# Sliding-window attention with a highway layer behind it: V's odd tiles copied to the other row half, PV in one phase, a narrower last stage, more biases by ScalarE, and a new order of steps

## The chip, the cores and the metric

The kernel runs on one core of a Trainium2 chip. The metric is device time in microseconds, from launch to end, of one execution. The engines are named as in the profile: PE (TensorE, matmuls), PEld (its weight loads), DVE (VectorE), ACT (ScalarE), POOL (GpSimd), SP (SyncE, which here only issues DMAs).

## The reference

Eight batches, eight heads, 576 positions, head width 64. Each query sees itself and the 127 keys before it, with a linear bias by distance that differs by head. The result of all heads, 4608 rows of 512, goes through a highway layer.

```
scores = (q @ k.T) / sqrt(64) - slope[h] * (i - j)       # where 0 <= i - j < 128
attn   = softmax(scores)                                  # else masked out
x      = (attn @ v), heads side by side                   # 4608 x 512
H      = relu(x @ w_h)
T      = sigmoid(x @ w_t + b_t)
out    = T * H + (1 - T) * x
```

## The kernel before, in words

**Steps and order.** The whole program is a string, `ORDER`, of three-character steps: a letter for the kind of step and a number for the item. A loop at the end reads it and emits the instructions of each step, under a manual schedule, so every engine gets its own instructions in the order in which the string names them. A second string, `BANKS`, gives the PSUM bank of each new accumulator (eight banks of 512 floats; `take`).

**Loading.** `L` steps load q and k of four heads of one batch (`ld..`), as bfloat16, from POOL's queue: four loads a batch (two groups of heads, k and q), 288 KB each. `V` loads V of a batch in 64-wide rows with a column of ones beside them (`va`, 576 KB), `W` the weights and the bias row, `B` the bias on all 128 rows (`bA`). A `T` step is one VectorE transpose of a load into `tr..`, so that the head width lies on 32 rows, two elements deep.

**Attention.** A batch has four stages; stage s holds the key tiles 2s and 2s+1 of 64 keys each, for all eight heads, and the fourth also tile 8. `s` computes the scores: 32 matmuls of 32 rows by 64 columns with 192 queries moving, and in the fourth stage 16 more of 32 by 128 with 64 queries. `e` is the exponential on ACT, from PSUM to bfloat16; `m` multiplies it on DVE by a table that holds both the distance bias and the mask (`mk`). In the probabilities the two tiles of a stage lie in different row halves, and which one is where alternates with the head, as V's rows do in memory (nine tiles a head). PV therefore runs in two phases: `p` for the even tiles, `y` (or `Y`, with a drain of PE ahead of it) for the odd ones, where the row halves change places. An output block is 128 queries; blocks of index NS hold the last 64 queries of two batches. `n` divides by the sum that the column of ones gave (a reciprocal and a multiply, on DVE).

**Highway layer.** For each of 36 blocks: `x` transposes the block on PE, `c` copies it to SBUF on ACT, `h` and `z` are four matmuls each with the two weights. The bias of the gate comes either by one more matmul at the end of `z` (L393), or by a copy of `bA` into the bank ahead of it on ACT (step `b`, 12 of the 36 blocks). `u` computes relu(h) - x on DVE; `U` is the relu on ACT and then needs `v`, the subtraction on DVE. `a` is a tanh on ACT; `t` (ACT) or `D` (DVE) turns it into the gate; `g` (DVE) or `G` (POOL) multiplies; `o` (POOL) or `O` (DVE) adds x; `d` stores from SP's queue. A POOL step of that kind waits for the DVE operation that the string names last before it.

Of the kernel before, what the change touches and what calls it, by code (L numbers as in the profile page):

```python
# [14 lines left out]
ADD = ()  # L15
# [3 lines left out]
    "Q00L00B00R00S00L01r00L02L03J00k00P00K00L04L05L06L07T00V00T01W00L08T02I00W01T03s00W02T04s"  # L19
    "01e00L09T05e01s02V01T06e02s03T07e03L10m00s04m01s05e04m02L11m03p00e05p01Y00Y01n00p02L12n0"  # L20
    "1x00Y02c00p03n02x01V02h00c01m04x02y03c02h01n03U00s06m05L13x03L14e06z00T08h02c03T09a00s07"
    "t00v00z01u01e07g00m06h03U02p04m07a01p05Y04t01Y05n04z02U03G01b03n05z03L15a02T10V03x04p06a"
    "03T11p07c04Y06t02Y07n06z04o01n07s08a04D03x05v02e08x06D04x07T12h04c05s09v03c06m08h05c07T1"
    "3G03e09z05u04G02h06U05T14a05s10o00b06p08T15e10Y08o03d00z06d01n08U06L16s11m09a06x08e11m10"
    "h07v05z07u07o02c08s12a07m11L17d02p09d03e12p10Y09Y10G04n09t05s13n10L18p11e13o04T16Y11x09x"
    "10L19c09n11d04s14c10V04h08m12e14h09m13U08s15m14b08h10e15g05T17o05z08u10z09a08d05v06t06m1"
    "5p12a09p13Y12t07x11n12U09z10G07c11T18t09x12y13o07a10p14p15n13Y14b11Y15L20c12v08p16n14t10"
    "G06z11n15h11a11o06T19x13x14c13y16L21d06p17c14n16d07L22x15h12L23c15D11g10U11s16D08U12g08y"
    "17v09z12e16n17G09T20x16h13a12o08c16s17b14u13z13L24d08e17v11L25m16z14t12T21o10p18a13s18a1"
    "4m17L26Y18t13h14n18e18G13z15T22o09U14p19a15s19b16v12V05d09Y19m18e19d10z16n19h15o13T23a16"  # L30
    "x17x18c17p20L27g12U15T24Y20G11c18s20z17n20e20o11T25h16o12t15d11s21a17u16x19e21d12h17D14v"
    "14d13m19h18U17z18c19T26G14U18x20m20L28h19a18c20D16s22T27b19G16p21e22Y21u19o14z19n21s23L2"
    "9v15d14a19m21L30p22e23h20g15D17z20m22U20v17x21m23p23c21p24y22a20Y23n22o15z21n23o16d15p25"
    "a21y24Y25t18n24G17p26d16t19x22n25h21c22L31v18x23x24U21v20y26g19x25b22D20h22g18c23g20n26o"
    "17z22t21c24u22h23V06a22d17v21c25s24T28U23z23e24O19h24D22O18a23m24s25d18b24d19h25e25v23D2"
    "3z24G23u25U24T29x26z25G22c26a24T30s26o20a25z26e26T31d20h26m25a26s27U26g21m26p27e27p28Y27"
    "Y28v24n27o21t24n28s28V07d21x27e28v26p29g24x28m27Y29c27s29c28n29o22h27e29h28m28d22U27p30o"
    "23u28s30b27Y30e30o24d23x29n30z27c29v27d24s31m29a27z28e31m30h29D26D25g26a28g25p31m31p32t2"
    "8x30z29c30D27U29g28g27p33a29o25y31y32n31h30b30n32d25x31z30c31O28p34O26a30y33Y34U30D29d26"
    "n33p35t30h31v29g29x32z31v30c32n34o29b32x33u31y35c33x34o27n35z32a31g30h32d27a32D31d28g31c"  # L40
    "34d29z33O30t32O31d30U32x35h33a33d31v32c35g32z34D33U33O32v33h34d32a34g33h35t34u34z35O33U3"
    "5g34d33v35O34a35D35d34g35O35d35"
)
BANKS = (
    "1404040642740106057405613572357067450674075047506406540540567507256320742534074507640674"
    "0671450740574357045064520326105307546054067150750640754076407605730625723310567540271570"
    "1"
# [3 lines left out]
def lists():  # L51
# [16 lines left out]
    by.update({k: blocks for k in "pynxchuvbzatgod"})  # L68
# [4 lines left out]
def kernel(  # L73
# [38 lines left out]
    TR = {(i, g, w): cp.tile([P, SQ, 2], BF16, name=f"tr{i}{g}{w}")  # L112
          for i in range(2) for g in range(NG) for w in "qk"}
    va = cp.tile([P, NB, NV, D + 1], BF16, name="va")
    VA = [va[:, i] for i in range(NB)]
    PB = [cp.tile([P, NH, 576], BF16, name=f"p{i}") for i in range(NP)]
    PE3 = [cp.tile([P, NH, 576], BF16, name=f"r{i}") for i in range(NP3)]
# [5 lines left out]
    MK = cp.tile([P, NH, 2, 192], BF16, name="mk")  # L123
    MA = cp.tile([P, NH, 2, 192], BF16, name="ma") if ADD else None
    MK3 = cp.tile([P, NH, 2, 256], BF16, name="mk3")
# [6 lines left out]
    scaled = [None]  # L132
# [4 lines left out]
    def between(ins, last=None):  # L137
        last = last or paired[0]
        if last is not None:
            tc.add_manual_dep(  # L140
                ins.ins, last.name,
                mybir.DependencyInfo(mybir.DependencyClass.Sync, mybir.DependencyReason.DATA),
                reason="starts behind VectorE's last operation on the shared port")
# [22 lines left out]

    def zero(ap):
        nc.vector.memset(ap.bitcast(U32), 0)  # L168

    def pads(i):  # L170
        for g in range(NG):
            for w in "qk":
                zero(TR[i, g, w][:, S:SQ, :])

    def clear(step):
        if step == "J":
            zero(spin[:])
        elif step == "R":
# [3 lines left out]
            pads(0)  # L182
        elif step == "P":
            for p in PB:
                for c in (0, 256, 512):
                    zero(p[:, :, c : c + 64])
        else:
            zero(ones0[:])
            nc.vector.memset(ones0[0:1, :], 1.0)
            for p in PE3:  # L190
                zero(p[:, :, 0:64])
            zero(MK3[:, :, :, 192:256])
            pads(1)
# [5 lines left out]
    def setup(step):  # L199
# [14 lines left out]
        elif step == "k":  # L214
            for tab in (MK, MK3):
                for h in range(NH):
                    for g in range(NG):
                        nc.scalar.activation(out=tab[:, h, g, 0:192], in_=rel[:], func=ACTF.Exp,
                                             scale=-slopes[4 * g + h])
            for half in range(2):  # L220
                rows = slice(half * D, (half + 1) * D)
                nc.scalar.copy(out=MK3[rows, half::2, :, 192:256], in_=MK[rows, half::2, :, 0:D])
        else:
            nc.sync.dma_start(
                out=bA[:], in_=moe_b_t.rearrange("(o n) -> o n", o=1).broadcast_to([P, DM]))

    def additive():
        for h in range(NH):
            for g in range(NG):
                nc.scalar.activation(out=MA[:, h, g, :], in_=rel[:], func=ACTF.Copy,  # L230
                                     scale=-slopes[4 * g + h] / scale)

    def tr(w, b, g):
        nc.vector.transpose(
            out=TR[b % 2, g, w][:, 0:S].rearrange("p s e -> p (s e)").bitcast(U32).rearrange(
                "p (s t) -> p t s", t=NT),
            in_=LD[b % 2, g, w][:].bitcast(U32).rearrange("p (t i) -> p t i", i=32))

# [15 lines left out]
    def scores(b, s):  # L254
# [3 lines left out]
        pitch = 192 if s < 3 else 256  # L258
        add = (b, s) in ADD
        for h in range(NH if add else 0):  # L260
            nc.tensor.matmul(
                out=sc[:, h, 0:384], lhsT=ident[:],
                rhs=MA[:, h].rearrange("p g n -> p (g n)"), start=True, stop=False)
        for g in range(NG):
            for e in range(2):
                for i in range(2):
# [35 lines left out]
    def terms(b, s, i):  # L302
        if s == NS:
            return [(3, 6, 128), (3, 8, 192)] if i == 0 else [(3, 7, 64)]
# [173 lines left out]
```

## Time and profile before

| | |
|---|---|
| median of 3 runs | 156.6 us (156.53 to 159.39) |
| the profiled execution | 156.13 us, of which the span is 154.2 |
| mean granted clock of PE | 0.976 |
| busy in the span: PE, DVE, ACT, POOL | 130.4, 136.0, 121.3, 80.8 us |
| DMA packets | 48106, 25.30 MB, 38224 of them under 512 B |
| last DVE operation ends / span ends | 149.9 / 154.2 us |

The profile counts an engine as busy while an instruction of it is under way; neighbours may overlap at their ends, so the distance from one start to the next is often shorter than an instruction. An idle time is named after what ended it. "Landing" is the time from the issue of a DMA to its completion.

### The profile page before, as it was taken

The numbers are of one execution on the slowest core, as the hardware profiler recorded it, in microseconds if no ns is written. First come the engines' busy times: TensorE is split into PE (matmuls) and PEld (weight loads), VectorE is DVE, ScalarE is ACT, GpSimd is POOL, SyncE is SP. The second block draws the span as 40 slices with busy tenths as digits, with TensorE's granted clock in tenths as the row PEclk, the third lists the DMA queues.
The fourth block names the chain that finished last, engine by engine and source line by source line (L and its number), as shares of the span: only waits on it lengthen the run. The fifth ranks groups of instructions, "written<-read, shape, count | busy, mean of one in ns | idle before, by whom it ended". The sixth has DMA issues, their size and how long they took to land.

```text
span 154.2 us, 6207 instructions
## 1 busy us (share of the span) xinstructions
PE 130.4 (85%) x2694; PEld 71.8 (47%) x2728; DVE 136.0 (88%) x257; ACT 121.3 (79%) x178; POOL 80.8 (52%) x90
## 2 busy tenths in 40 slices
PE   0598658698998999998999999989999799999930
PEld 0233326344554555465545545466445554555410
DVE  4999948398999899997999999989999979999880
ACT  3655972299579999994999999868999999868830
POOL 6984414402909479279488957554753771204000
PEclk9999995999999999999999999999999999999995
DMA  4999999999999759997999998786599199042732
GB/s 70 197 206 207 161 198 210 160 196 167 189 175 65 197 107 204 189 185 142 127 223 231 221 183 232 137 161 168 101 129 229 68 133 233 6 138 108 302 136 68
DMA packets 48106, 25.30 MB, mean 164 GB/s; under 512 B 38224, under 2 KB 39248, under 8 KB 48080
## 3 DMA queue, kind: packets, MB, share of 16 engines
q0 software_dynamic: 42688, 15.21, 91.6%
q1 hardware_dynamic: 5392, 9.70, 18.5%
q8 instruction: 21, 0.34, 0.9%
q14 instruction: 5, 0.04, 0.1%
HBM read 30.67 MB, written 9.44 MB: 260 GB/s over the span
## 4 chain that ended last, share of the span: by engine, by line
PE 70%; DMA 10%; issue 6%; DVE 6%; ACT 5%; DVEq 0%
PE ps L389 19%; PE ps L362 19%; PE ps L333 14%; DMA va<-in_v_dram 10%; PE ps L269 8%; PE ps L352 6%; PE ps L393 3%; ACT r L293 2%; ACT p L293 1%; DVE ot L417 1%; PE ps L279 1%; DVE p L168 1%; DVE uu L412 0%; DVE x L343 0%; ACT tt L402 0%
## 5 line engine op out<-in xcount | busy, mean ns | idle before, releaser
L417 POOL TENSOR_TENSOR ot<-uu,x 128x512 f32<-128x512 bf16 x26 | 29.8, 1155 | 23.8 <-DVE uu L376 9.6
L293 ACT ACTIVATE p<-ps 128x1536 bf16<-128x1536 f32 x24 | 34.7, 1457 | 4.6 <-PE ps L269 4.3
L362 PE MATMUL ps<-wH,xt 128*128 128x512 bf16 x130 | 35.3, 382 | 1.6 <-issue 1.0
L389 PE MATMUL ps<-wT,xt 128*128 128x512 bf16 x127 | 35.4, 380 | 1.1 <-issue 0.3
L412 POOL TENSOR_TENSOR uu<-uu,tt 128x512 bf16<-128x512 bf16 x14 | 16.1, 1153 | 23.8 <-ACT tt L402 10.6
L357 ACT COPY xt<-ps 128x512 bf16<-128x512 bf16 x36 | 20.6, 587 | 9.9 <-PE ps L352 9.7
L397 ACT ACTIVATE tt<-ps 128x512 f16<-128x512 f32 x36 | 21.6, 602 | 7.0 <-PE ps L393 4.7
L343 DVE TENSOR_TENSOR x<-ps,rd 128x512 bf16<-128x512 f32 x36 | 24.9, 691 | 2.1
L333 PE MATMUL ps<-va,p 64*128 64x65 bf16 x768 | 22.2, 193 | 3.9 <-DMA va<-in_v_dram 1.3
L300 DVE TENSOR_TENSOR p<-p,mk 128x1536 bf16<-128x1536 bf16 x24 | 22.8, 970 | 0.0
L333 PEld LDWEIGHTS <-p 64*128 64x128 bf16 x768 | 16.6, 95 | 12.6 <-issue 10.2
L362 PEld LDWEIGHTS <-xt 128*128 128x128 bf16 x144 | 13.0, 99 | 14.2 <-issue 1.8
L389 PEld LDWEIGHTS <-xt 128*128 128x128 bf16 x144 | 12.6, 98 | 12.9 <-issue 0.6
L154 POOL DMA_DIRECT2D va<-in_v_dram x8 | 14.8, 1851 | 1.9 <-DMA ld00k<-in_k_dram 1.0
L293 ACT ACTIVATE r<-ps 128x2048 bf16<-128x2048 f32 x8 | 15.0, 1874 | 0.5
L372 ACT ACTIVATE uu<-ps 128x512 bf16<-128x512 f32 x24 | 14.4, 604 | 1.0 <-PE ps L362 0.9
L352 PE MATMUL ps<-ident,x 128*128 128x128 bf16 x144 | 13.7, 225 | 1.5 <-issue 1.2
L342 DVE RECIPROCAL rd<-ps 128x8 f32<-128x8 f32 x36 | 7.1, 198 | 7.6 <-PE ps L333 7.1
L352 PEld LDWEIGHTS <-x 128*128 128x128 bf16 x144 | 9.5, 99 | 6.3 <-issue 1.9
L402 ACT ACTIVATE tt<-tt 128x512 f16<-128x512 f16 x19 | 11.9, 632 | 0.1
L242 PE MATMUL ps<-spin 128*128 128x512 bf16 x22 | 7.2, 503 | 5.4 <-DVE spin L168 5.4
L300 DVE TENSOR_TENSOR r<-r,mk 128x2048 bf16<-128x2048 bf16 x8 | 10.3, 1294 | 0.3 <-ACT r L293 0.3
(77 smaller groups left out, 195.2 us busy)
## 6 DMA issues: line engine op xcount, KB each, us to landing
out_dram<-ot SPq DMA_DIRECT2D x32, 256.0 KB, 4.0
va<-in_v_dram POOLq DMA_DIRECT2D x8, 576.0 KB, 10.9
ld00k<-in_k_dram POOLq DMA_DIRECT2D x4, 288.0 KB, 5.7
ld00q<-in_q_dram POOLq DMA_DIRECT2D x4, 288.0 KB, 6.0
ld01k<-in_k_dram POOLq DMA_DIRECT2D x4, 288.0 KB, 6.1
ld01q<-in_q_dram POOLq DMA_DIRECT2D x4, 288.0 KB, 7.1
ld10k<-in_k_dram POOLq DMA_DIRECT2D x4, 288.0 KB, 5.8
ld10q<-in_q_dram POOLq DMA_DIRECT2D x4, 288.0 KB, 7.5
```

What stands on the lines that cost most here:

```text
L154: ins = nc.gpsimd.dma_start(out=va[:, b, :, 0:D], in_=v[b].rearrange("h s d -> (h s) d").rearrange("(n p) d -> p n d", p=P))
L293: nc.scalar.activation(out=pview(b, s), in_=SC.pop((b, s))[:, :, 0:n].rearrange("p h (g n) -> p h g n", g=NG), func=ACTF.Exp, scale=scale)
L300: alone(nc.vector.tensor_tensor(out=p, in0=p, in1=(MK3 if s == 3 else MK)[:], op=ALU.mult))
L333: mm = nc.tensor.matmul(out=av[o : o + m, par, j * (D + 1) : (j + 1) * (D + 1)], lhsT=PT[bb, st][rows, h, c : c + m], rhs=VA[bb][rows, at ...
L343: nc.vector.tensor_tensor(out=x[:].rearrange("p (i r d) -> p r i d", i=NH, r=2), in0=av[:, :, :, 0:D], in1=rd[:].to_broadcast([P, 2, NH, D ...
L352: nc.tensor.transpose(out=pt[:, c * P : (c + 1) * P], in_=X[b, s][:, c * P : (c + 1) * P], identity=ident[:])
L357: nc.scalar.copy(out=xt[:].rearrange("p c n -> p (c n)"), in_=XP.pop((b, s)))
L362: nc.tensor.matmul(out=pa, lhsT=XT[b, s][:, c, :], rhs=wH[:, c, :], start=c == 0, stop=c == NC - 1)
L389: nc.tensor.matmul(out=pz, lhsT=xt[:, c, :], rhs=wT[:, c, :], start=c == 0 and not given, stop=c == NC - 1 and given, skip_group_check=given)
L397: nc.scalar.activation(out=tt[:], in_=PZ.pop((b, s)), func=ACTF.Tanh, scale=0.5)
L412: note(eng.tensor_tensor(out=uu, in0=uu, in1=TT.pop((b, s))[:], op=ALU.mult))
L417: note(eng.tensor_tensor(out=ot[:], in0=UU.pop((b, s))[:], in1=X[b, s][:], op=ALU.add))
```

## The change

- Heads are grouped by parity: group g holds heads g, g+2, g+4, g+6, and its scores for every tile go to row half g. Both groups share one `tr` tile.
- Of V, the even-numbered tiles of a head already lie in that half, the odd-numbered ones in the other. A new step `X` copies those, four tiles a head, to `vo` in the right half, by two DMAs of 64 rows on SP's queue for each batch.
- PV has one phase (`p`), with no drain, in the order head, tile, row half.
- The fourth stage has 448 score columns a head instead of 512, all by 32x64 matmuls. Its exponential goes to a tile of its own (`e..`), and the mask becomes two instructions (768 and 1024 columns). The two mask tables become one, computed in 8 activations with the slope as a per-row scale instead of 16.
- Other counts: bias copies (`b`) 12 to 32, and bias matmuls 24 to 4; `u` 12 to 28, `U` and `v` 24 to 8; `t` 19 to 24, `D` 17 to 12; `G` 14 to 18, `g` 22 to 18; `o` 26 to 29, `O` 10 to 7; PE drains 25 to none.
- The last block's `h`, `u`, `g`, `O` and `d` run in two halves of 256 columns (second halves: `f`, `w`, `q`, `j`, `l`), and its second rows are stored from ACT's queue.
- `ORDER` and `BANKS` are new. V of batch 0 stands third in POOL's queue, behind ld00k and ld00q; before it stood ninth. The iota stands behind eight DMA issues instead of one. `bA` is loaded behind batch 0's transposes.

```
 ORDER = (
-    "Q00L00B00R00S00L01r00L02L03J00k00P00K00L04L05L06L07T00V00T01W00L08T02I00W01T03s00W02T04s"
...
+    "L00R00L01P00V00J00K00L02L03L04L05L06S00L07r00Q00k00T00X00T01L08W00T02I00W01T03W02s00V01T"
+    "04s01e00T05L09s02m00e01L10T06e02s03T07e03m01p00n00s04m02s05e04m03T08p01e05x00n01c00m04s0"
...
-                out=LD[b % 2, g, kind][:],
-                in_=(q if kind == "q" else k)[b, 4 * g : 4 * g + 4].rearrange(
-                    "h (s t) d -> (h s) (t d)", t=NT))
+                out=LD[b % 2, g, kind][:], in_=(q if kind == "q" else k)[b, g::NG].rearrange(
+                    "h (s t) d -> h s (t d)", t=NT))
...
+    def across(b):
+        for g in range(NG):
+            n = 5 * g
+            nc.sync.dma_start(
+                out=VO[b][g * D : (g + 1) * D].rearrange("p h n e -> p h (n e)"),
+                in_=va[(1 - g) * D : (2 - g) * D, b].rearrange("p (h m) e -> p h (m e)", h=NH)[
+                    :, :, n * (D + 1) : (n + NH) * (D + 1)])
...
+        for i in range(3 if s == 3 else 2):
+            t, n = 2 * s + i, 192 if i < 2 else D
             for e in range(2):
+                for g in range(NG):
                     for h in range(NH):
+                        rows = slice(32 * h, 32 * h + 32)
                         nc.tensor.matmul(
+                            out=sc[g * D : (g + 1) * D, h, 192 * i : 192 * i + n],
+                            lhsT=TR[b % 2, "k"][rows, g * S + t * D : g * S + (t + 1) * D, e],
+                            rhs=TR[b % 2, "q"][rows, g * S + t * D : g * S + t * D + n, e],
+                            start=e == 0, stop=e == 1, tile_position=(32 * h, g * D))
...
+        e3 = E3[b % 2]
+        nc.vector.tensor_tensor(out=p[:, :, 0, 0:192], in0=e3[:, :, 0:192], in1=MK[:, :, 0, 0:192], op=ALU.mult)
+        alone(nc.vector.tensor_tensor(out=p[:, :, 1, :], in0=e3[:, :, 192:448], in1=MK[:, :, 1, :], op=ALU.mult))
...
-        elif fence:
-            nc.tensor.drain()
...
+        for h in range(NH):
+            for n, (st, t, c) in enumerate(ts):
                 for r in range(2 if s == NS else 1):
...
+                    for g in range(NG):
+                        rows = slice(g * D, (g + 1) * D)
+                        nc.tensor.matmul(
+                            out=av[o : o + m, g, h * (D + 1) : (h + 1) * (D + 1)],
+                            lhsT=PT[bb, st][rows, h].rearrange("p i n -> p (i n)")[:, c : c + m],
+                            rhs=VO[bb][rows, h, t // 2, :] if t % 2 else va[rows, bb, (9 * (NG * h + g) + t) // 2, :],
+                            start=h == 0 and n == 0, stop=h == NH - 1 and n == len(ts) - 1)
...
+            eng = nc.scalar if r and (b, s) == LAST else nc.sync
+            eng.dma_start(out=out[row : row + D, at], in_=ot[r * D : (r + 1) * D, at])
```

More of the change, by code (lines that the diff above doesn't have):

```diff
@@ L265, in scores @@
             for e in range(2):
-                for i in range(2):
+                for g in range(NG):
                     for h in range(NH):
-                        rows, half, t = slice(32 * h, 32 * h + 32), (h + i) % 2, 2 * s + i
+                        rows = slice(32 * h, 32 * h + 32)
                         nc.tensor.matmul(
-                            out=sc[half * D : (half + 1) * D, h, g * pitch : g * pitch + 192],
-                            lhsT=TR[b % 2, g, "k"][rows, t * D : (t + 1) * D, e],
-                            rhs=TR[b % 2, g, "q"][rows, t * D : t * D + 192, e],
-                            start=e == 0 and not add, stop=e == 1 and (g == 1 or not add), tile_position=(32 * h, half * D))
@@ L319, in pv @@
+    def pv(b, s):
+        av = AV[b, s] = take(2)
+        ts = terms(b, s)
+        for h in range(NH):
+            for n, (st, t, c) in enumerate(ts):
                 for r in range(2 if s == NS else 1):
@@ L426, in store @@
             row = (2 * b + r) * S + 512
[L427 to L429 removed]
+            eng = nc.scalar if r and (b, s) == LAST else nc.sync
+            eng.dma_start(out=out[row : row + D, at], in_=ot[r * D : (r + 1) * D, at])
+    second = dict(f=mm_h, w=lambda b, s, half: relu_sub(b, s, "u", half), l=store,
+                  q=lambda b, s, half: gate(b, s, "g", half), j=lambda b, s, half: add_x(b, s, "O", half))
+    do = dict(L=load, V=load, W=load, X=lambda w, b: across(b), b=bias, T=tr, s=scores, e=soft, m=mask, p=pv, n=norm, x=x_tr, c=x_copy, h=mm_h,
               u=relu_sub, v=sub_x, z=mm_z, a=tanh, t=to_gate, g=gate, o=add_x, d=store)
```

244 lines of the change are left out of this document (103 added, 141 removed).

## The prediction

> **What bounds the kernel now.** First the page: busy times, the slices, the chain that ended last.
>
> ```profile
> span 154.2 us, 6207 instructions
> PE 130.4 (85%) x2694; PEld 71.8 (47%) x2728; DVE 136.0 (88%) x257; ACT 121.3 (79%) x178; POOL 80.8 (52%) x90
> ...
> PE   0598658698998999998999999989999799999930
> ...
> DVE  4999948398999899997999999989999979999880
> ...
> PEclk9999995999999999999999999999999999999995
> ...
> PE 70%; DMA 10%; issue 6%; DVE 6%; ACT 5%; DVEq 0%
> ```
>
> Three parts are seen: a start with holes (DVE's 4, 8, 3 in slices 6 to 8, about 19 to 31 us), a dense middle, and a tail. The chain runs over PE for 70%, but in the middle DVE is just as full. I therefore cut the span into stretches, and asked what DVE waits for in the dense one (columns of the first: span, then busy us and instructions of PE, PEld, DVE, ACT, POOL, the granted clock, DMA share, GB/s).
>
> ```profile
> 22.00:31.00 9.00, 6.92 (x163) 4.59 (x164) 4.75 (x10) 2.56 (x5) 3.96 (x5) 0.81 1.70 187
> ...
> 40.00:147.00 107.00, 101.17 (x2167) 56.94 (x2192) 101.33 (x182) 95.05 (x137) 61.64 (x60) 1.00 1.01 163
> ```
> ```profile
> DVE rd L342 <- PE ps L333: 2.1, 4, 0.7
> DVE uu L368 <- PE ps L362: 0.4, 1, 0.4
> DVE rd L342 <- ACT tt L397: 0.4, 1, 0.4
> DVE tt L404 <- ACT tt L397: 0.4, 1, 0.4
> DVE uu L376 <- ACT uu L372: 0.2, 1, 0.2
> ```
>
> From 40 to 147 us DVE is busy 101.3 of 107 us, PE 101.2, ACT 95.1. Of DVE's 5.7 idle us only 3.5 are waits that another engine ends; the rest is the short step between a reciprocal and the multiply behind it. So relieving PE alone can give the middle 3.5 us at most, unless DVE also gets less to do. The start hangs on a load:
>
> ```profile
> 6.80 15.12 DMA va<-in_v_dram
> 22.06 0.55 PE ps L333 x24
> ```
>
> V of batch 0 is issued behind all eight q and k loads and lands at 21.9; only then does PV begin. (Landings here and below are the issue plus the time to landing, from the views of the single loads' tiles.)
>
> **The change part by part.** Prices on DVE and ACT are start to start, since an instruction's end overlaps the next:
>
> ```profile
> 33.58 0.41 DVE L376 TENSOR_TENSOR uu<-uu,x 128x512 bf16<-128x512 bf16 x1
> 33.91 0.67 DVE L368 SCALAR_TENSOR_TENSOR uu<-ps,x 128x512 bf16<-128x512 f32 x1
> 34.51 0.40 DVE L412 TENSOR_TENSOR uu<-uu,tt 128x512 bf16<-128x512 bf16 x1
> 34.83 0.94 DVE L300 TENSOR_TENSOR p<-p,mk 128x1536 bf16<-128x1536 bf16 x1
> ```
>
> This gives v (subtract) 0.33, u (relu and subtract from PSUM) 0.60, g (gate) 0.32. In the same way: mask 0.86, transpose 1.09, reciprocal with multiply 0.85, scaling of the gate D 0.20, add O 0.60. ACT's relu, bias copy and scaling take 0.48, 0.50 and 0.53 (means of 604, 601 and 632 ns, less the overlap).
>
> *PE, middle.* Bias matmuls fall from 24 to 4: 20 x 0.21 (the chain's step for one) = -4.3. The 25 fences between the halves of PV go: the chain shows 0.12 and 0.16 of "issue" at two of them near 136 us, 25 x 0.14 = -3.5. In eight last stages the 32x128 shape goes (some 0.15 each): -1.2. In all -9.0. The order of the score matmuls also changes; the count does not, and I price it at 0 (32 take 0.48 or 0.59 in the chain now; 0.11 more on all 32 stages would be 3.5, and 0.11 less a gain of as much: neither moves DVE's load).
>
> *ACT, middle.* Copies of the bias 12 to 32: 20 x 0.50 = +10.0. Relus (U) 24 to 8: 16 x 0.48 = -7.7. Scalings (t) 19 to 24: 5 x 0.53 = +2.7. Last stage 2048 to 1792 columns: (1874 - 1457) / 512 = 0.81 ns a column, x 256 x 8 = -1.7. Sum +3.3, so 98.4 where 95.1 were.
>
> *DVE, middle.* u 12 to 27 whole and 2 half ones: 15 x 0.60 + 0.7 = +9.7. v 24 to 8: -5.3. D 17 to 12: -1.0. Gates 22 to 17 whole and 2 half: -1.2. Adds 10 to 6 whole and 2 half: -1.7. The mask of a last stage becomes two instructions of 768 and 1024 columns: no row has them; between 1.13 x 1792 / 2048 = 0.99 (by columns) and 1.27 (the rows of 512 and 1536 give 0.56 and 0.70 by a straight line, nothing overlapped), against 1.13 now, 8 times: -1.1 to +1.1. I take -0.5, as overlap is what the rows show. Sum 0.0: **the engine that is fullest gets no lighter.** POOL takes 4 more gates and 3 more adds, 7 x 1.15 = +8.1 of 61.6 in 107, and has room.
>
> So the middle can only gain by fewer waits. I take 2.0 of the 3.5 us as gone: the 2.5 that end on PE largely, those on ACT not, as ACT gets fuller. Bounds 0 and 3.5.
>
> *The copies (X).* Sixteen transfers of 133 KB on SP's queue, each pair waiting for V's load. SP issues in order, so the stores of finished blocks stand behind that wait, and an add that needs the buffer of a block six earlier would wait for them; V lands a batch ahead, which hides it. No on-chip transfer is in the trace; the 128 KB stores land in 2.4 us, V's own loads in 10.9, and a pair of copies should land between. As load on the DMA engines a pair costs between 1.3 us (rate of the q and k loads, which landed 1.4 us apart) and 2.6 (rate of V: 5.8 from the landing of the last k/q load at 16.1 to its own at 21.9). I take 1.3: runs of 520 bytes are nearer to wH's 1024-byte ones, which moved at the k/q rate. In the middle it is hidden by loads that run a batch or more ahead; without that cover 6 x 1.3 = 7.8 would show.
>
> *The start.* V is now third in POOL's queue, so the loads behind it land 5.8 later, and those behind the first pair of copies 1.3 more: k and q of batch 0's second group at 14.8 and 16.2 (9.1 and 10.5 before), the last of batch 1 at 23.1 (16.1). The iota also moves behind eight DMA issues, so its three DVE steps end near 8.8 instead of 5.1; the wait for 14.8 hides that. First scores near 17.4 (12.6 before), T07 done at 24.3 (17.4). DVE in its new order then has 11.7 us without a wait I can find (five masks 4.3, two of last stages 2.1, four norms 3.4, T08 1.1, a u 0.6, a D 0.2); T09 and T10 wait a little for their loads (36.2 and 37.6, V of batch 1 now being ahead of them too), done at 38.7. Before, T10 was done at 40.16 with 2.15 us more of other work done by then (two norms, a v and a g more, a D less). 1.46 us are left between the two: **0.7 behind**, not 5, because the old start lost the time at V instead. Removed memsets (10 x 0.14) and half of the mask table (8 x 0.26 on ACT) fall into waits: 0. Bounds -0.6 (V holds the queue for only 5.1, which is what is left if wH behind it took the 2.5 of wT, and the copies cost nothing) and +3.0 (T09 to T11 late too, as one of their loads now stands behind POOL's first gate).
>
> *The tail.* The last block's second half is issued by SP and ACT at once: one issue of 0.56 less (1.12 for two now); the doubled gate and add cost about 0.2: -0.4, bounds -0.8 and +0.2.
>
> **The sum.** The profiled execution took 156.13: the span and 1.93 around it. 156.13 + 0.7 - 2.0 - 0.4 = 154.4; the runs' median is 0.3% above that execution, so 154.9. Over 2% is what a measurement can tell from no change (3.1 us).
>
> **Rivals.**
>
> *PE was the bound (faster).* For it: 70% of the chain, and 2.4 us of named PE waits in the middle. Then all 3.5 us go, the start comes out at -0.6 and the tail at -0.8: 156.13 - 4.9 = 151.2, 151.7 as a median. Against it: DVE's waits don't hold more.
>
> *ACT becomes the bound (slower).* Place: 40 to 147 us. ACT keeps its 12 idle us (11.0 of them are named waits for PE, on tt and xt), because a copied bias must come ahead of its matmuls and holds a PSUM bank from there to the tanh; then its +3.3 lengthens the middle: 156.13 + 3.3 + 0.7 - 0.4 = 159.7, 160.2 as a median. It decides from the point where ACT cannot get its idle time under 9 us. For it: DVE and ACT wait on each other inside every block. Against: what ACT waits for is PE, which gets 9 us lighter.
>
> *A cold start that is not made up (no change or little slower).* PE has some 6 us between its warm-up spins and the first scores. In the trace a pause from 20.8 to 22.06 was followed by a granted clock of 0.81 over 22 to 31, and four transposes took 0.61 instead of 0.40. Four stages, each with 0.48 of scores and 0.43 of fill, would double to 1.8, 0.3 more than an exponential: +1.2, and with the start's upper bound of 3.0, nothing gained in the middle, -0.4: 156.13 + 3.8 = 159.9 at worst, 158 at half of it. [...]
>
> **Chances.** Forecast 0.45 (own range 153.0 to 156.8), PE the bound 0.27, ACT the bound 0.13, cold start 0.15. Faster by over 2% (under 153.5) takes the first rival and 0.03 of the forecast: 0.30. Slower (over 159.7) takes 0.12 of ACT and 0.05 of the cold start: 0.17. The rest, 0.53, lies within. Range 151.2 to 159.6: from the first rival to just under ACT's price.
>
> **What would show it.** Right: DVE over 96% busy in the middle with under 2 us of waits on PE; ACT's share up to 92% or more; first scores near 17, first PV near 24, L393's successor with 4 matmuls. Wrong: first scores before 15 (V costs less than 5.8), DVE busy time in the middle off 101 by more than 2, waits of PE or DVE on the copies, or ACT with 12 idle us as before.

## The result, and the profile after

The changed kernel takes **189.13 us** (188.63 to 190.0) where the kernel before takes 156.77: a ratio of 1.208 (95% interval 1.201 to 1.214). 154.9 was forecast, in a range that ended at 159.6. Some of the kernels below vary by 5 to 10 us from one execution to the next, so ratios are formed from undisturbed executions alone and can lie below the ratio of the medians; where none is given, the lowest time stands beside the median.

The page of the changed kernel, with the rows that answer to those shown of before:

```profile
span 188.1 us, 6224 instructions
...
PE 138.8 (74%) x2712; PEld 75.3 (40%) x2712; DVE 133.4 (71%) x249; ACT 122.4 (65%) x178; POOL 92.9 (49%) x97
...
PE   0960193997037997499579995992699998999970
...
DVE  4170477897332994895749996697468997999991
...
PEclk9997567599955999859969998899699999999999
...
DMA packets 64907, 27.48 MB, mean 146 GB/s; under 512 B 50800, under 2 KB 56176, under 8 KB 64880
...
q0 software_dynamic: 54976, 15.26, 113.4%
...
DMA 51%; PE 26%; POOL 7%; DVE 6%; issue 4%; ACT 3%; SPq 1%; DVEq 0%; ACTq 0%; POOLq 0%
```

DVE's busy total has even fallen (136.0 to 133.4); PE's has grown by 8.4 us and POOL's by 12.1, far less than the 32 us that the kernel takes longer. What grew is the holes. The first slices of PE read 0, 9, 6, 0, 1, and holes come back through the first three quarters of the span, each with a lower granted clock in the slice behind it (5 to 8 tenths in the row PEclk). The chain, 70% PE before, is 51% DMA. The queue of POOL's loads (q0) has 12288 packets more than before, for nearly the same bytes. Its row of before:

```profile
q0 software_dynamic: 42688, 15.21, 91.6%
```

The windows (columns as in the prediction), then what DVE waits for from 40 to 180 us, and PE's longest wait there:

```profile
22.00:31.00 9.00, 5.91 (x149) 2.74 (x149) 6.18 (x7) 5.91 (x4) 3.75 (x4) 0.69 1.24 181
40.00:180.00 140.00, 114.80 (x2364) 63.89 (x2363) 106.92 (x190) 104.58 (x156) 78.47 (x74) 0.90 1.33 146
```
```profile
DVE rd L317 <- PE ps L307: 21.7, 10, 5.8
DVE tr1q L233 <- DMA ld11q<-in_q_dram: 4.3, 2, 3.3
DVE tr0k L233 <- DMA ld01k<-in_k_dram: 1.8, 1, 1.8
```
```profile
PE ps L307 <- DMA vo<-va: 17.4, 7, 6.8
```

Before, DVE waited 2.1 us for PV in the dense part; here 21.7. PV in turn waits for the copies, as the chain of the changed kernel shows in order of time (start, us, what; the short steps between these are left out):

```profile
2.92 16.89 DMA va<-in_v_dram
20.67 11.03 DMA vo<-va
44.66 12.09 DMA bA<-in_moe_b_t_dram
71.30 16.86 DMA va<-in_v_dram
88.81 6.53 DMA vo<-va
110.65 16.91 DMA va<-in_v_dram
128.27 5.08 DMA vo<-va
146.25 9.92 DMA ld11q<-in_q_dram
```

V lands after 16.9 us, its copies 5 to 11 us later; the load of the bias, behind the second pair of copies in SP's queue, is issued at 44.7 and keeps ACT waiting 11.2 us. The loads of q, k and V have all become slow, V's too, whose form the change does not touch. From the page's part on DMA issues, of before and then of after (KB each, median us to landing):

```profile
va<-in_v_dram POOLq DMA_DIRECT2D x8, 576.0 KB, 10.9
ld00k<-in_k_dram POOLq DMA_DIRECT2D x4, 288.0 KB, 5.7
```
```profile
va<-in_v_dram POOLq DMA_DIRECT2D x8, 576.0 KB, 16.9
vo<-va SPq DMA_DIRECT2D x16, 130.0 KB, 5.3
ld00k<-in_k_dram POOLq DMA_DIRECT2D x4, 288.0 KB, 10.6
```

### The profile page after: what moved, and what is told of

The parts are those of the page before. It is cut to its first block, busy times and chain, and to the rows that moved or that the text cites. A ratio compares the mean times of both kernels' runs of the same rounds, so it can differ in the third digit from the quotient of the medians.

```text
span 188.1 us, 6224 instructions
## 1 busy us (share of the span) xinstructions
PE 138.8 (74%) x2712; PEld 75.3 (40%) x2712; DVE 133.4 (71%) x249; ACT 122.4 (65%) x178; POOL 92.9 (49%) x97
## 3 DMA queue, kind: packets, MB, share of 16 engines
q0 software_dynamic: 54976, 15.26, 113.4%
## 4 chain that ended last, share of the span: by engine, by line
DMA 51%; PE 26%; POOL 7%; DVE 6%; issue 4%; ACT 3%; SPq 1%; DVEq 0%; ACTq 0%; POOLq 0%
DMA va<-in_v_dram 27%; DMA vo<-va 12%; PE ps L374 8%; DMA bA<-in_moe_b_t_dram 6%; PE ps L345 6%; DMA ld11q<-in_q_dram 5%; PE ps L307 5%; PE ps L265 3%; PE ps L327 3%; POOL ot L405 2%; ACT e L279 2%; POOL uu L398 1%; POOL ld00q L148 1%; SPq L169 1%; DVE ot L405 1%
## 5 line engine op out<-in xcount | busy, mean ns | idle before, releaser
L405 POOL TENSOR_TENSOR ot<-uu,x 128x512 f32<-128x512 bf16 x29 | 33.1, 1151 | 36.8 <-DVE uu L398 10.0
L374 PE MATMUL ps<-wT,xt 128*128 128x512 bf16 x144 | 41.7, 421 | 2.3 <-ACT ps L365 2.1
L398 POOL TENSOR_TENSOR uu<-uu,tt 128x512 bf16<-128x512 bf16 x18 | 20.6, 1150 | 34.4 <-DVE tt L389 15.8
L345 PE MATMUL ps<-wH,xt 128*128 128x512 bf16 (+1 forms) x148 | 37.5, 381 | 0.1
L307 PE MATMUL ps<-vo,p 64*128 64x65 bf16 x384 | 20.3, 203 | 20.3 <-DMA vo<-va 20.2
L307 PEld LDWEIGHTS <-p 64*128 64x128 bf16 x768 | 17.8, 102 | 31.6 <-issue 30.9
L365 ACT COPY ps<-bA 128x512 f32<-128x512 f32 x32 | 18.9, 601 | 11.5 <-DMA bA<-in_moe_b_t_dram 11.2
L307 PE MATMUL ps<-va,p 64*128 64x65 bf16 x384 | 20.4, 204 | 1.6 <-issue 1.0
L354 DVE SCALAR_TENSOR_TENSOR uu<-ps,x 128x512 bf16<-128x512 f32 (+1 forms) x29 | 19.1, 663 | 0.4 <-PE ps L345 0.4
L265 PE MATMUL ps<-tr0q,tr0k 32*64 32x192 bf16 (+1 forms) x576 | 10.4, 260 | 10.3 <-DVE tr0q L233 10.2
L327 PE MATMUL ps<-ident,x 128*128 128x128 bf16 x144 | 15.5, 239 | 3.1 <-DVE x L318 2.6
L387 ACT ACTIVATE tt<-tt 128x512 f16<-128x512 f16 x24 | 15.1, 642 | 0.1
L327 PEld LDWEIGHTS <-x 128*128 128x128 bf16 x144 | 10.7, 106 | 10.8 <-issue 3.7
## 6 DMA issues: line engine op xcount, KB each, us to landing
va<-in_v_dram POOLq DMA_DIRECT2D x8, 576.0 KB, 16.9
ld00k<-in_k_dram POOLq DMA_DIRECT2D x4, 288.0 KB, 10.6
ld01q<-in_q_dram POOLq DMA_DIRECT2D x4, 288.0 KB, 12.1
```

The lines of the kernel that those rows point to most:

```text
L307: nc.tensor.matmul(out=av[o : o + m, g, h * (D + 1) : (h + 1) * (D + 1)], lhsT=PT[bb, st][rows, h].rearrange("p i n -> p (i n)")[:, c : c ...
L327: nc.tensor.transpose(out=pt[:, c * P : (c + 1) * P], in_=X[b, s][:, c * P : (c + 1) * P], identity=ident[:])
L345: nc.tensor.matmul(out=pa, lhsT=XT[b, s][:, c, :], rhs=wH[:, c, at], start=c == 0, stop=c == NC - 1)
L354: nc.vector.scalar_tensor_tensor(out=uu, in0=pa, scalar=0.0, in1=X[b, s][:, at], op0=ALU.max, op1=ALU.subtract)
L374: nc.tensor.matmul(out=pz, lhsT=xt[:, c, :], rhs=wT[:, c, :], start=c == 0 and not given, stop=c == NC - 1 and given, skip_group_check=given)
L398: note(eng.tensor_tensor(out=uu, in0=uu, in1=TT[b, s][:, at], op=ALU.mult))
```

## The experiments

### The loads' form

The prediction had passed over one edit: the q and k loads take every second head, `q[b, g::NG]` as `"h s (t d)"`, in place of four neighbouring heads as `"(h s) (t d)"`. The source rows of four neighbouring heads lie at one step, 128 of them; those of every second head are 4 x 32. Theory A: this form alone makes the loads slow. Theory B, its rival: the way from V's load over the copy to PV holds the kernel up, whatever the loads do. The form was put into the kernel before (`b_strided`) and taken out of the changed one (`a_contig`); two more took the copies out, by loading V straight into the halves, with the slow form (`a_direct`) and with the old one (`a_both`).

```
b_strided: -  q[b, 4 * g : 4 * g + 4], "h (s t) d -> (h s) (t d)"
           +  q[b, g::NG],             "h (s t) d -> h s (t d)"
a_contig:  the reverse, in the changed kernel
a_direct:  + V of heads 4g..4g+3 by a load of its own, 64 rows, into row half g; no copies
a_both:    a_direct with a_contig's loads, heads side by side throughout
```

> The kernel before with one thing of the change added: each q and k load takes every second head (the heads are then grouped otherwise than the rest of the kernel takes them; every instruction keeps its shape). No copies, no new order. Theory A: the first load takes about 9.4 us to land, DVE gets waits on loads that it had not, and the time rises to 165 to 185 us. Theory B: 155 to 160, as before.

> The changed kernel with one thing undone: each q and k load takes four heads that lie side by side, as before, instead of every second head, so that the 128 rows of its source are one run of equal steps again (the heads' work is otherwise left as it is, so each row group works on another head than the change gives it; every instruction keeps its shape). Theory A (the load of every second head is spread over only a quarter of the DMA engines, and starves everything behind it; its first load took 9.4 us to land instead of 4.9): the first load lands 4.9 us after its issue again, V's loads land in 11 us rather than 17, PV's waits on the copies fall from 20 us to under 5, and the time is 153 to 161 us. Theory B (the chain from V's load over the copy to PV is what holds it up, whatever the loads do): PV still waits over 12 us for the copies, time over 175.

> The changed kernel without the copies: V is loaded from memory straight into the row half where PV wants it, by two loads of 64 rows in place of one of 128 (heads of V grouped side by side, those of q and k as in the change; every instruction of the other engines keeps its shape). The q and k loads still take every second head. Theory A: V still lands late behind them, PV waits on V instead of on the copies, time 175 to 190. Theory B: the wait for the copies is gone, time 153 to 162.

> The changed kernel with both undone: heads side by side in a group throughout (loads, slopes, V, the place of a head in x), V loaded straight to its row half by two loads of 64 rows, no copies. Theory A: 152 to 158, and within 3 us of the run that only mends the loads, since the copies cost little once V is on time. Theory B: the same as the run without copies, since the loads would not matter. If neither load form nor copies explain the 32 us, this one stays over 165.

Measured: `b_strided` 187.17 (ratio 1.183, 1.176 to 1.191), `a_contig` 160.72 (1.016, 1.012 to 1.020), `a_direct` 209.37 (1.323), `a_both` 173.92 (1.097, 1.089 to 1.104). The form by itself costs the kernel before 30 us, and taking it out gives the changed kernel 28 back; theory B falls. In `b_strided` DVE waits 19.6 us for q and k loads at its transposes (0.4 before) and 15.6 for PV (7.1 before). q0 has 54976 packets in `b_strided` and 42688 in `a_contig`.

`a_direct` and `a_both` missed what was hoped of them. V by two loads of 64 rows is slower than V by one load and copies. In the packet records of the trace a 128-byte packet, of which V's loads consist, takes 121 ns (median) in `a_both` and 32 in `a_contig`, at the same number of packets. Whether the 64 rows, the two loads at once or the order of the pieces within a load makes a packet four times as long was not separated.

What is it in the form? The extra packets are 4 bytes long, 384 for each of the 32 loads: 12 x 32. The author's estimate from that count: of the 16 DMA engines on the page 4 carried the data, 32 runs each, as many as the outermost count of the source, and the other 12 had a filler for each run. To tell that from "any broken run is slow", the next kernel breaks the run at another place:

```
b_outer2 (from before):
-  (q)[b, 4 * g : 4 * g + 4].rearrange("h (s t) d -> (h s) (t d)")
+  (q)[b].rearrange("(x g y) s d -> g x y s d", x=2, g=NG)[g].rearrange("x y (s t) d -> x (y s) (t d)")
```

> The kernel before, its q and k loads taking heads 2g, 2g+1, 4+2g and 5+2g in place of 4g to 4g+3 (so the groups hold other heads than the rest of the kernel takes them for): the same bytes and the same 1152-byte runs, the source now 2 x 64 runs where the kernel with every second head had 4 x 32. Theory (the number of DMA engines that carry a load follows the outermost count of its pattern): 2 engines carry it, the first load of q or k lands some 64 x 0.19 + 3.3 = 15 to 16 us after its issue, a software queue of 45,000 + 2 x 32 x 12 more small packets at most, and the time is over 200 us. Rival (any source that is not one even run costs the same, whatever its outermost count): the first load lands after 9.4 us as with 4 x 32, and the time is 184 to 190.

Measured: 214.72 us in one execution. The page of `b_outer2`:

```profile
q0 software_dynamic: 71360, 15.32, 96.2%
...
ld00k<-in_k_dram POOLq DMA_DIRECT2D x4, 288.0 KB, 15.8
```

71360 is 42688 + 32 x 14 x 64, what two engines with 64 runs each and 14 with fillers would give. The landing goes 5.7, 10.6, 15.8 us for outermost counts of 128, 4 and 2, though `b_outer2` has longer unbroken stretches than the changed kernel. The rival falls: in these kernels the landing goes with the outermost count. (Two figures of the expectation were wrong: the extra packets are 14 x 64 a load, not bounded by 2 x 32 x 12, and the runs are of 2304 bytes, not 1152.)

That a load has fewer packets under way, and not that the fillers take the time, can be read from the packet records. In the kernel before, while its first loads follow each other (5 to 14.5 us), 17.4 packets of 2304 bytes are under way at once. In `b_strided` the number stands most often at 4.4 (26.0 to 28.5 us, for one), a quarter of that; in `b_outer2` at 2.2 (28.5 to 30.0 us), 4.4 and 6.7, an eighth and its multiples. If 17.4 are what 16 engines have under way, one load has 4 of them in the one kernel and 2 in the other, as estimated from the fillers. With several such loads at once 17.8 are under way again (`b_strided`, 9 to 10 us); what grows is the landing of each (ld00k: 10.3 us there, 5.7 before).

### The copies

`a_contig` is 4 us above before by the medians, not below. Its waits:

```profile
DVE rd L317 <- PE ps L307: 10.5, 8, 4.2
PE ps L307 <- DMA vo<-va: 8.3, 5, 5.1
```

Three theories of what the copies cost: PV waits for them (C); their share of the DMA engines makes all loads later (D); later a third, F, below. `a_fix` makes the mended kernel whole, with heads side by side throughout and the copies in runs of 2340 bytes; `a_fix_v5` moves V of batch 5 ahead; `a_fix_v5_v9` puts V of batch 0 back behind the eight loads; `a_nocopy` has `a_contig`'s loads and no copies.

```
a_fix:        + rows of group g hold heads 4g..4g+3 in slopes, PV and norm; VO[b] = 64 runs of 18 tiles
a_fix_v5:     + V05 ahead of L23 in ORDER
a_fix_v5_v9:  + V00 ahead of r00
a_nocopy:     - X steps;  rhs = va[rows, bb, (9 * (NG * h + g) + t) // 2, :]   for every tile
```

> The changed kernel with heads side by side in a group throughout (loads, slopes, place in x), and V still copied on chip: the 18 tiles that a half lacks then lie in one run, so a copy is 64 runs of 2340 bytes instead of 256 of 520. Order of steps unchanged. Theory A (the form of the q and k loads was the 32 us; the copies ride along): as the run that only mended the loads, 158 to 161. If the short runs of the copies matter, 2 us or more under it.

> As a_fix, with V of batch 5 issued 47 steps earlier in the order (step V05 ahead of L23). With the loads mended, one stall of 5.1 us of PE on a copy was left near 103 us: V of batch 5 was issued at 83.3, landed at 95.9 and its copy at 103.0. Theory C (what is left above the old kernel is this one late load, in a chain made longer by the copy): that wait is gone, PE waits under 2 us for copies after 40 us, and the time falls by 3 to 5 us, to 154 to 157. Rival D (what is left is spread: ACT fuller, the start slower): it falls by under 1.5 us.

> As a_fix_v5, with V of batch 0 back behind the eight q and k loads (step V00 ahead of r00), so that only this placement differs. Theory E (V in third place costs the start under 1 us, since the old start lost it at V instead): within 1 us of a_fix_v5, with first scores 3 us earlier and first PV 3 us or more later. Rival (scores 3 us late are not made up): 2 to 4 us faster than a_fix_v5.

> The changed kernel with the q and k loads mended as in a_contig, without the copies: PV takes every tile of V from the loaded tile, in whichever row half it reads (so half of the tiles of V it uses are others); every instruction of the engines keeps its shape. The price of the copies when the loads are on time: theory A together with C says 3 to 6 us under a_contig, 153 to 157, as the copy's 4 to 11 us are no longer between V and PV. If the copies are hidden: as a_contig, 158 to 161.

Measured: `a_fix` 162.98 (lowest 158.01), `a_fix_v5` 161.59 (lowest 157.33; ratio 1.012, 1.006 to 1.018), `a_fix_v5_v9` 163.30 (lowest 159.67), `a_nocopy` 151.09 (0.962, 0.953 to 0.972). **Without copies and with the old loads, the rest of the change is a gain of 3.8%.** That is a time only: `a_nocopy` leaves out putting the odd tiles of V into the right rows, so its result is of no use, and the same holds for the kernels made from it below. It is 9.6 us under `a_contig`, where 3 to 6 were expected. V in third place costs nothing that can be seen, nor do the longer runs of the copies in `a_fix` bring anything. Advancing one V brings 1.4 us by the medians, 0.7 by the lowest times, which is within the scatter.

Is the rest of the gain the new order and the copied biases? `b_order` gives these to the kernel before, with its own layout and PV. `a_early` moves the bias load and V of batches 3 to 7 ahead in `a_fix`.

```
b_order (from before):  ORDER and BANKS of after without X, p and y issued together with a drain between,
                        32 of 36 biases by ACT, last block in halves
a_early (from a_fix):   B00 ahead of L09; V03, V04, V05, V06, V07 ahead of L17, L22, L23, L26, L31
```

> The kernel before with its own loads, V as it lands, PV in its two phases with the fence between them and the 512-column last stage, but with the new order of steps (less the copies), 32 biases by ScalarE and the last block in halves. Theory (the load's form and the copies are what was lost, the order and the biases are the gain): 151 to 153.5 us, ratio 0.96 to 0.98, since the variant without copies ran 151.1 and this one puts back 3.5 us of fences and 1.2 of 32x128 matmuls on PE, of which part shows. Rival (the gain of the variant without copies lay in PV without phases and in the shorter last stage, the order alone brings nothing): 155.5 to 158.

> The changed kernel with heads side by side throughout, and the loads of V of batches 3 to 7 and of the bias each issued two to five loads earlier than in the new order. Theory C (the copies' cost is lateness: V and copies land too late for their PV): under 155, with waits of PE on the copies under 1 us. Theory D (the copies' cost is their share of the DMA engines and the spread that they cause, wherever V is issued): 157 to 161 in the fastest run, since V earlier makes a q or k load later by the same time.

Measured: `b_order` 159.96 (ratio 1.011, 1.001 to 1.020), `a_early` 163.17 (lowest 159.30). Both hopes fell: the order brings nothing by itself, and with V brought forward three of four q and k loads into the first buffers come later (ld00k, ld00q and ld01k land in 8.3, 9.5 and 11.2 us in `a_early`, in 6.9, 6.4 and 7.7 in `a_contig`; ld01q in 6.8 and 8.4), as the rivals had it (`b_order` is even above its rival's 155.5 to 158). `b_order` has a fence in all 36 blocks, where before has 25; at the 0.15 us a fence measured below, the eleven more are 1.7 us.

Two kernels then separate the copies' transfers from the waits for them: `a_unread` makes the sixteen transfers and reads none, `a_pool` makes the copies on GpSimd without a transfer.

```
a_unread (from a_nocopy):  + X steps as in a_contig
a_pool (from a_fix):       -  nc.sync.dma_start(out=VO[b][...], in_=va[...])
                           +  between(nc.gpsimd.tensor_copy(out=VO[b][...], in_=va[...]));   X00 ahead of p00
```

> The variant without copies (151.1), with the sixteen copies put back at their places but read by nobody: PV still takes every tile of V as it landed (so odd tiles are those of other rows). Theory C (the copies cost because PV waits for them): 150.5 to 153, no more than the variant without them. Theory D (their share of the DMA engines and of SP's queue is the cost, by making q, k and V land later): 157 to 161, as with copies that are read (160.7).

> The changed kernel with heads side by side throughout and the sixteen copies made by GpSimd (64 rows of 1170 elements each, in to one half from the other) in place of transfers; the first pair stands right ahead of PV of batch 0. If the copies cost by their transfers (theory D, or the landing time of theory C), this loses them: 151 to 155, with POOL's busy time up by 16 x 1.2 to 2.0 = 19 to 32 us from 88.6. Rival (POOL cannot take them: its gates and adds come late, and its queue holds back the loads): over 157.

Measured: `a_unread` 158.95 (1.015, 1.010 to 1.021), `a_pool` 171.97 (1.099, 1.094 to 1.105). The first seemed to settle for D: 7.9 us for transfers that nobody reads. Its trace says otherwise. The chain of `a_unread`, then the stretch from 40 to 50 us in it and in `a_nocopy`:

```profile
15.85 16.52 DMA va<-in_v_dram
32.39 0.59 SPq L169
33.02 1.07 SPq L169
34.14 8.59 DMA bA<-in_moe_b_t_dram
42.83 0.60 ACT ps L365
```
```profile
40.00:50.00 10.00, 6.15 (x83) 3.46 (x85) 3.17 (x5) 5.17 (x9) 0.70 (x1) 0.66 1.41 144
```
```profile
40.00:50.00 10.00, 9.77 (x228) 5.08 (x234) 9.12 (x15) 9.74 (x15) 6.63 (x10) 1.00 1.58 196
```

The bias load stands in SP's queue behind the second pair of copies, which wait for V of batch 1. It lands at 42.7; ACT cannot copy a bias into a bank before (one wait, 7.8 us), and all engines stop: DVE is busy 3.2 of 10 us there, against 9.1. That is theory F. In `a_nocopy` the same load was issued at 15.5.

`a_pool` loses on the engines. A copy takes POOL 1.16 us, cheap enough; but it waits in POOL's queue for V (12.7 us in five waits), with the loads behind it, and DVE's busy time rises. Its page:

```profile
PE 132.4 (77%) x2676; PEld 73.5 (43%) x2712; DVE 147.7 (86%) x249; ACT 122.2 (72%) x178; POOL 110.3 (65%) x113
```

DVE has the same 249 instructions as in `a_nocopy`, where they took 131.4 us. Set against the medians of the same instructions in `a_nocopy`, DVE's take 14.3 us longer, of which 7.2 lie on instructions that overlap a copy; what makes the others longer stays open.

The last runs test F, and mend what can be mended.

```
a_unread_b (from a_unread):  B00 ahead of L09
a_contig_b (from a_contig):  B00 ahead of L09
a_fix_b2 (from a_fix_v5):    B00 ahead of L09, V01 ahead of W01
a_fix_b3 (from a_fix_v5):    B00 ahead of L09, V03 ahead of L17
```

> The variant whose copies nobody reads (158.95; PV takes odd tiles of V as they landed), with the load of the bias moved ahead of the second pair of copies in SP's queue. Theory F (of the 7.9 us that unread copies cost, nearly all is the bias load, which stands in SP's queue behind the second pair of copies and so behind V of batch 1: 34.1 issued, 42.7 landed, ACT's one wait for it 7.8): 151 to 152.5. Theory D (the transfers' share of the DMA engines): 157 to 159.

> The variant with mended loads whose copies are read (160.7; its row groups hold other heads than the rest takes them for), with the bias load moved as in the run beside it. Theory F with C (what is left of the copies' cost is PV's wait for a V that lands too late, 8.3 us of PE's waits in five places there): 158 to 160, since the bias load was not waited for there, PV's wait for the copies coming last. If the bias load was the cost here too: 152 to 154.

> The changed kernel with heads side by side throughout, V of batch 5 ahead of load 23, the bias load ahead of the second pair of copies, and V of batch 1 ahead of the second weight's load. If V's lateness (theory C) and the bias load (F) are what was left: 152 to 155. If not: 157 to 160, as with V of batch 5 alone (157.3 at its best).

> The changed kernel with heads side by side throughout, V of batch 5 ahead of load 23, the bias load ahead of the second pair of copies, and V of batch 3 ahead of load 17, where V of batch 1 keeps its place. V of batch 3 and its copies ended the wait of PE in the middle in three of these runs (issued 51 to 55, copied by 69 to 71). If that wait is what is left (theory C): 153 to 156. If a V moved forward only makes a q or k load late in its place (theory D): 157 to 160.

Measured: `a_unread_b` 152.92 (0.973, 0.966 to 0.981), `a_contig_b` 161.43 (lowest 154.89), `a_fix_b2` 160.47 (1.011, 1.005 to 1.016), `a_fix_b3` 159.16 (lowest 153.68). F is shown for unread copies: moving one load gives 6.0 of the 7.9 us back, and 1.8 are left for the transfers themselves, a difference that the noise of the two kernels covers. With copies that are read, the bias load was not what came last (`a_contig` has no wait for it), and moving it does not lower the median. The waits for copies stay (8.2 us in `a_contig_b`), or something else takes their place. In `a_fix_b2`, where V of batch 1 overtook the second weight:

```profile
DVE rd L315 <- PE ps L305: 6.2, 5, 4.3
PE ps L372 <- DMA wT<-in_moe_w_t_dram: 3.1, 1, 3.1
DVE tr1q L231 <- DMA ld11q<-in_q_dram: 2.7, 2, 2.1
...
PE ps L305 <- DMA vo<-va: 0.9, 1, 0.9
```

The wait on copies is down to 0.9 us, and 3.1 for the weight and 2.7 for a q load stand there instead. We read this as C and D being two sides of one thing for copies that are read: all loads come from one queue, the DMA engines are 90% busy or more in `a_contig` from 4 to 106 us (but for 31 to 39 us, at 70% or more), and whichever load is put last is waited for. No run shows it by itself. `a_fix_b3` reached 153.7 once; what separates that execution from the one of 162.3 stays open. None of the versions whose copies are read is measurably faster than the kernel before.

### PE or DVE

`b_order`'s miss points to PE: it has the order of `a_nocopy`, but fences between the halves of PV. So 36 fences (drains of PE) were put into `a_nocopy`.

```
a_nocopy_fence:      for h in range(NH):
                +        if h == 2: nc.tensor.drain()
```

> The variant without copies (151.1; PV takes odd tiles of V as they landed), with one fence of PE put into the middle of each of the 36 blocks' PV. The prediction held that relief of PE brings at most 3.5 us, as DVE is the fuller engine. By it the fences (36 x 0.14 = 5.0 us of PE) cost little: 151 to 152.5. Rival (PE and DVE are equally full and every us of PE is on the path, which would also explain why the kernel before with the new order and its own PV ran no faster): 154.5 to 157.

Measured: 157.64 (ratio 0.997, 0.992 to 1.001, against 0.962 without fences): 3.4% or 5.4 us (6.5 by the medians), 0.15 us a fence, the full price. The page's totals and the dense part with DVE's longest waits, of `a_nocopy` and then of `a_nocopy_fence`:

```profile
PE 125.9 (85%) x2712; PEld 69.4 (47%) x2712; DVE 131.4 (89%) x249; ACT 121.2 (82%) x178; POOL 88.6 (60%) x97
```
```profile
40.00:140.00 100.00, 96.46 (x2142) 53.99 (x2140) 95.67 (x172) 96.69 (x146) 68.31 (x67) 1.00 1.24 170
```
```profile
DVE rd L317 <- PE ps L307: 0.5, 2, 0.3
```
```profile
PE 130.2 (84%) x2712; PEld 70.9 (46%) x2712; DVE 132.9 (86%) x249; ACT 122.1 (79%) x178; POOL 88.6 (57%) x97
```
```profile
40.00:140.00 100.00, 93.83 (x2044) 51.30 (x2043) 91.16 (x159) 91.66 (x136) 65.65 (x65) 1.00 1.19 157
```
```profile
DVE rd L319 <- PE ps L309: 4.2, 8, 1.1
DVE uu L356 <- PE ps L347: 1.9, 1, 1.9
```

In this stretch all engines are less busy with fences, PE too, and DVE's wait for PV goes from 0.5 to 4.2. Over the whole span PE's busy total rises from 125.9 to 130.2 for the same 2712 matmuls (those of PV alone from 25.8 to 32.2), so most of a fence's price is counted as busy time. The expectation that fences would cost little falls: in this kernel a microsecond of PE is a microsecond of the whole.

## Why the prediction was wrong, step by step

**The step that failed: "those behind the first pair of copies 1.3 more", with loads taken at the old rate.** The start and the cover of the copies were worked out with "the rate of the q and k loads, which landed 1.4 us apart", as if `g::NG` changed nothing. The edit stood in the diff and no term of the sum has it. With that form 4.4 large packets of a load are under way (`b_strided`) where 17.4 were, and a load lands in 10.6 us in place of 5.7: +28 to +30 us in all. That is 28.4 of the 32.4 us lost; the rest belongs to the copies, and with the loads mended `a_contig`, at 160.7, still lies above the end of the range. Before has no load in that form, so its trace could not price the edit; a run of the form alone, `b_strided`, could.

**The copies.** "V lands a batch ahead, which hides it" was wrong twice. Landing after V was bounded by 2.4 and 10.9 us; the median was 5.3 in the changed kernel (11.0 at worst) and 3.9 with mended loads, within the bounds. But V is not a batch ahead: in `a_contig` V of batch 5 was issued at 83.3 and copied at 102.9, and PV waited 5.1 us there. And what stands behind the copies on SP was named as stores alone; the bias load, 32 of whose copies now stand ahead of matmuls, was not. Copies cost 9.6 us (160.7 to 151.1). That the prediction has 7.8 "without that cover" is near by luck: it was the price of their load on the DMA engines, which showed as some 1.8 (`a_unread_b`); most of the rest fits the 8.3 us that PE waits for copies in `a_contig`.

**What bounds the kernel: "DVE is just as full".** By busy time this holds (101.2 and 101.3 of 107 us). What relief of PE alone would bring in the kernel before, 3.5 us at most by the prediction, no run measures. With fences DVE waits 6.1 us for PE (4.2 and 1.9 above), and taking the fences out brought 5.4, so there the waits were a fair bound. In three kernels the time goes with PE's load rather than DVE's: PE's busy total is 130.4 us before, 125.9 in `a_nocopy` and 130.2 with the fences, DVE's is 136.0, 131.4 and 132.9, and the ratios are 1, 0.962 and 0.997. That speaks for PE as the bound, but does not settle it: the start differs as well, and no run adds a known cost to DVE alone. Rival 1, "PE was the bound", gave 151.7; without the loads' form and the copies the kernel takes 151.1. That it is so near is luck in part, since the start and DVE's load were not as that rival had them.

**DVE, "sum 0.0".** DVE's total is 131.4 in `a_nocopy`, 4.6 less than before. By busy time of the rows u is +10.8 (predicted +9.7), v -6.9 (-5.3), D -1.5 (-1.0), gates -1.6 (-1.2), adds -1.8 (-1.7), masks -0.8 (-0.5): -1.8. Memsets, said to fall into waits, are another -1.7. The rows count overlaps that the prediction's start-to-start prices leave out, so they can't be set against these one by one; but the total, which counts an overlap once, says that the fullest engine did get lighter, where the sum had 0.0. POOL's +8.1 measured +7.8. The mask's two halves, 0.55 and 0.68 us by mean, add up to 1.23 against 1.29 for one, near the chosen end.

**Waits in the middle, "2.0 of 3.5".** From 40 to 140 us DVE's named waits on engines fell from 2.9 to 0.7 in `a_nocopy`: 2.2 gone, as forecast. But 1.9 us of waits on loads are new there.

**The start.** +0.7 was swamped: but for four matmuls at 13.8, the first scores came at 22.6, not 17.4. That V stands third was not the reason, as `a_fix_v5_v9` shows. With the old loads and no copies (`a_nocopy`) the start was better than forecast: scores at 15.5, and T10 done at 36.3 where 38.7 was forecast. By the prediction's own comparison that is 1.7 us ahead of before, beyond its bound of -0.6. The two loads forecast to land at 14.8 and 16.2, behind V, were being transposed from 12.7 and 14.2, so V held them for less than the 5.8 that was priced. The cold start's low granted clock did appear (0.69 from 22 to 31 us), but behind loads; with the loads on time, in `a_nocopy`, it is 0.82 from 12.5 to 22 us and 1.00 from 22 to 31. The doubling in that rival's price is borne out: before shows a granted clock of 0.50 from 24 to 27 us, and in the changed kernel a stage of scores with its fill took 1.76 us at 0.50 (24.36 to 26.12), where 1.8 was priced. How long a pause has to be for that, no run shows.

**ACT as the bound** did not come as a longer time: its total is 121.2 in `a_nocopy`, 121.3 before, with 32 bias copies. Yet from 40 to 140 us it is as full as PE there (96.7 and 96.5 us of 100; DVE 95.7), as the prediction's sign of 92% or more had it.

Of "what would show it wrong", the waits on the copies and DVE's busy time in the middle both did; the loads' landing, which came first, was not on that list.

## What to carry to other kernels

Price every edit of a transfer's pattern, even one that moves the same bytes in the same run length: look at the outermost count first, since 4 in place of 128 cost this kernel 18% and 2 cost 37% (one execution). When a wait is put on a queue, list everything behind it, one-off loads included: here a load of one bias row, stuck behind a copy that nobody read, cost 6 us. Two engines at 95% by busy time are told apart by adding a known cost to each in turn; here that was done for PE alone, so it is known that PE's time counts, and not that DVE's does not.

## What had not been expected of the hardware

- A load whose outermost count is 4 left 384 packets of 4 bytes beside its 128 of 2304, one of count 2 left 896; their landing rose by 4.9 and 10.1 us, and 4.4 and 2.2 of the large packets were under way at once, where 17.4 were before.
- V by loads of 64 rows: 121 ns for a 128-byte packet where the 128-row load shows 32, and 173.9 us for a kernel without copies against 160.7 with them.
- A copy of 64 x 1170 elements between row halves takes GpSimd 1.16 us, but in that kernel 249 DVE instructions took 147.7 us, not 131.4.
- 36 drains of PE cost 5.4 us, and PE's busy total rose by 4.3 with them.
- The kernels that wait on loads vary by up to 10 us between executions (`a_contig_b` 154.9 to 165.1), the kernel before by 1 to 3.
